# A chunked recurrence and an MLP in one kernel: tables of powers applied by TensorE products for two chunks, and a remainder of x taken by a product with minus one

## The chip, the cores and the metric

The kernel runs on one core of one Trainium2 chip. The time is that of one execution on the device, in microseconds (us); a measured time is the median of several executions. The profile is of one execution, and its span is the time from the first to the last instruction.

## The reference, cut to what matters

```python
# r, k, v: (B=4, H=8, S=768, D=48); w in 0.85..0.95 and u: (8, 48)
for t in range(S):
    cur = einsum('bhd,bhe->bhde', u * kt, vt)
    y[:, :, t] = einsum('bhd,bhde->bhe', rt, state + cur)
    state = w * state + einsum('bhd,bhe->bhde', kt, vt)
x = y as (3072 tokens, 384)
h = x @ w_in                      # 384 x 2048
g = max(h, 0) + alpha * min(h, 0)
out = g @ w_out                   # 2048 x 384
```

## The kernel before

The 768 time steps are cut into C = 6 chunks of L = 128 tokens. A chunk of all four batches is NT = 512 columns. Heads are taken in P = 4 pairs q; the two heads of a pair lie on partitions 0 to 47 and 64 to 111 of a 112-row tile.

**The recurrence.** For a pair (c, q) the tiles `r` and `k0` hold r and k with the feature on the partitions and (batch, token) in the free dimension. VectorE multiplies them by rows of powers of w (the tables `W[q]`). Their products per batch give scores; a mask (`copy_predicated`) and a diagonal term (`base`) make the matrix that is multiplied with `v`. The state `T[q]` (feature by feature, per batch) needs k a second time, with the token on the partitions: the tile `k`, shape [128, 2*B, D]. It is loaded from DRAM (`kk<-vkr`) and multiplied on VectorE by a table of powers by token, `scale_k` at L382: `wtok` for chunk 0, `whalf` for the later chunks, which work in two halves of 64 tokens. `token_table` and `half_table` make these tables by ScalarE copies (L275, L292), TensorE transposes (L279, L296) and one VectorE copy (L282, L299). Chunk 0 is handled by `first_chunk`, where `state` issues the load of k (L447), scales it and makes U (L457). The pairs of chunks 1 to 5 are handled by `prepare` and `burst`; `hasty` marks chunk 1. One burst is one block of TensorE work: the earlier pair's output y through the state (L569) and through the scores (L579), then this pair's products (L543, L550); the rest of y's products (`through_scores(1)`) follow after a small ScalarE read, `seen_y` (L592).

**x as two parts.** The MLP runs on fp32r operands, and each operand is split in a high part and the rest: `xh` and `xl` for x, `wh` and `wl` for the weights, `gh` and `gl` for g. In `burst` the function `splits` does this for y by four quarter blocks of 48 partitions by 256 columns: ScalarE copies a block of PSUM to `xh` (L361) and VectorE subtracts, xl = y - xh (L362). Some rows of x are then moved between partitions by small DMAs (`lower`, L350).

**The MLP.** A step is one chunk with one 128-wide slice i of the hidden layer: 9 products of 128 x 512 into a bank (`m_in`, L628), ScalarE and VectorE work for g, gh and gl (L636, L637, L640, L641), and 9 products into three accumulators (`m_out`, L661). The steps run as chunk 0 with slices 0 to 8, chunk 1 with slices 0 to 8, chunk 0 and then chunk 1 with slices 9 to 15, and then chunks 2 to 5. Each slice of weights comes as one load of 768 KB into `wraw`, which has two buffers, and is unpacked and split by ScalarE (L326, L336) and VectorE (L328, L330, L333, L337); L330 and L333 are the last to read `wraw`, and the load two slices on waits for them.

**The order.** Every piece of work is registered with an engine, an estimated time, what it reads and writes and a rank; `in_order` plays this through as a list schedule and gives one order for all engines. The engines run their queues in that order. SP issues all loads, in order as well. Five PSUM banks are handed out by the schedule, three more are the accumulators; other tiles rotate over a fixed number of buffers (raw 6, v 4, kk 3). Where the schedule leaves TensorE a gap in the start-up, short products on `ident` (`warm`, L721) are put in.

Of the kernel before, what the change touches and what calls it, by code (L numbers as in the profile page):

```python
# [18 lines left out]
L = 128  # L19
# [48 lines left out]
class Plan:  # L68
# [108 lines left out]
def rwkv_prelu_kernel(ctx: ExitStack, tc, rk, vkr, wP, uP, u, wall, alpha, w, r_all, k_all, v_all, oT):  # L177
# [13 lines left out]
    def sb(shape, name, bufs, dt=F32):  # L191
        return plan.buf(lambda: wk.tile(shape, dt, name=name, bufs=bufs), name, bufs)
# [16 lines left out]

    W = [fixed([112, L + 1], f"W{m}") for m in range(P)]  # L210
    w128, unit = fixed([112, P], "w128"), fixed([112, 65], "unit")
    wtok = sb([128, H, D], "rr", 1)

    T = [None] * P

    uw = fixed([112, P, 2], "uw")
    wh, wl = ([fixed([128, 2 * NK, 128], f"{n}{i}", F32R) for i in range(NF)] for n in ("wh", "wl"))
    flag = fixed([1, 1], "flag", I32)

    bank = pb([128, NT], "acc2")  # L220
    plan.banks += [ps.tile([128, NT], F32, name=f"bank{i}") for i in range(5)]

    def psum(group=None, bufs=0):
        return Bank(plan, group, bufs)


    def half(h):
        return slice(HI * (h % 2), HI * (h % 2) + D)
# [40 lines left out]
            out=w128()[:, m:m + 1], in0=t()[:, 128:129], in1=t()[:, 128:129], op=ALU.mult), r=[t], w=[(w128, m)],  # L269
            rank=-31)  # L270

    def token_table():
        rows, pt = sb([112, P, L], "g", 3), psum()
        for m in range(P):
            add("ACT", 0.4, lambda m=m: nc.scalar.activation(  # L275
                rows()[:, m], W[m]()[:, L - 1::-1], AF.Copy, scale=w128()[:, m:m + 1]), r=[W[m], (w128, m)],
                w=[(rows, m)], rank=-30)
        for m in range(P):
            add("PE", 0.15, lambda m=m: nc.tensor.transpose(  # L279
                pt()[:, 128 * m:128 * m + 112], rows()[:, m], ident()[0:112, 0:112]),  # L280
                r=[(rows, m), ident], w=[(pt, m)], rank=-30)
        add("DVE", 0.4, lambda: nc.vector.tensor_copy(  # L282
            wtok().rearrange("p (m g) e -> p m g e", g=2),
            pt()[:, :].rearrange("p (m g e) -> p m g e", m=P, g=2)[:, :, :, 0:D]), r=[pt], w=[wtok], rank=-30)

    def half_table():

# [99 lines left out]

    def first_chunk(q):
        r, k0 = (sb([112, B, L], *(("o", 2) if q == P - 1 else ("raw", 6))) for _ in range(2))
        v, k = sb([128, 2 * B, D], "v", 4), sb([128, 2 * B, D], "kk", 3)  # L390
        n = 2 * B * D
        inputs(0, q, r, k0, v, k, -99 + 0.1 * q)
        first_k.append(k0)
        first_v.append(v)
        if q == P - 1:
            raw_weights(0, -97, [k0])
            raw_weights(1, -95, [v])
        for j, (t, tab) in enumerate(((r, lambda: W[q]()[:, None, 0:L]), (k0, lambda: W[q]()[:, None, L - 1::-1]))):
            add("DVE", 0.72, lambda t=t, tab=tab: nc.vector.tensor_tensor(
                out=t(), in0=t(), in1=tab().broadcast_to([112, B, L]), op=ALU.mult),  # L400
                r=[W[q]], w=[t], rank=10 * q + j - 90)
        cu = sb([128, 2, B], "cu", 2)
        diagonal(q, r, k0, cu, bank, slice(8 * q, 8 * q + 8), (bank, q), 10 * q - 88, -90.2 + q, -51 + q)

        A = [psum() if q % 2 == 0 else pb([128, NT], f"acc{g}") for g in range(2)]

        def scores():
            for b in range(B):
                for g in range(2):
                    nc.tensor.matmul(A[g]()[:, b * L:(b + 1) * L], k0()[half(g), b], r()[half(g), b], start=(b == 0),  # L410
                                     stop=(b == B - 1), skip_group_check=True)

        add("PE", 1.1, scores, r=[r, k0], w=A, rank=10 * q - 90)
        base = [sb([128, B, L], "gl" if q % 2 else "base", 3) for _ in range(2)]
        for g in range(2):
            for b in range(B):
                add("ACT", 0.39, lambda g=g, b=b: nc.scalar.activation(
                    base[g]()[:, b], ident(), AF.Copy, scale=cu()[:, g, b:b + 1]), r=[cu, ident], w=[(base[g], b)],
                    rank=-50.9 + q)
        for g in range(2):  # L420
            add("DVE", 0.75, lambda g=g: nc.vector.copy_predicated(
                base[g](), strict()[:, None, :].broadcast_to([128, B, L]),
                A[g]()[:, :].rearrange("p (b t) -> p b t", b=B)), r=[strict, A[g]], w=[base[g]],
                rank=10 * q - 76 + g)
        y = psum()

        def out():
            for b in range(B):
                for g in range(2):
                    rows, x = (slice(0, HI) if g == 0 else half(g)), g * B + b  # L430
                    nc.tensor.matmul(y()[rows, b * L:(b + 1) * L], v().rearrange("p x e -> p (x e)")[
                        :, x * D:x * D + rows.stop - rows.start], base[g]()[:, b], start=b == 0,
                        stop=b == B - 1, skip_group_check=True)

        add("PE", 1.0, out, r=[v] + base, w=[y], rank=10 * q - 90)
        h, l, kx = x_tiles(0, q)
        if q < P - 1:
            splits(kx, h, l, y, lambda: y()[0:112, :], slice(0, 112), slice(0, NT), [0, 2, 3, 4, 5], 0.6, q - 51.2)
        if q:
            lower(0, q - 1)  # L440
        if q == P - 1:
            for g in range(2):
                splits(kx, h, l, y, lambda g=g: y()[half(g), :], half(g), slice(0, NT), [2 + 2 * g, 3 + 2 * g], 0.6,
                       q - 51.2)

        def state():
            load(k, lambda: nc.sync.dma_start(k().rearrange("p x e -> p (x e)"), vkr[0, q, :, n:2 * n]), 192,  # L447
                 -20 + q, [first_v[P - 1]])
            U = psum()
            add("DVE", 0.56, lambda: scale_k(k, wtok, q), r=[wtok], w=[k], rank=0.5 * q - 1)  # L450

# [12 lines left out]
        return state  # L464
# [20 lines left out]
    def prepare(c, q, at):  # L485
        hasty = c == 1
        r, k0 = (sb([112, B, L], "raw", 6) for _ in range(2))
        v, k = sb([128, 2 * B, D], "v", 4), sb([128, 2 * B, D], "kk", 3)
        n, early = 2 * B * D, at - 7
        inputs(c, q, r, k0, v, k, early)  # L490
        load(k, lambda: nc.sync.dma_start(k().rearrange("p x e -> p (x e)"), vkr[c, q, :, n:2 * n]), 192,
             early + 0.1 * q + 0.2)


        for t, tab in ((r, lambda: W[q]()[:, None, 0:HI]), (k0, lambda: W[q]()[:, None, L - 1:HI - 1:-1])):
# [20 lines left out]
        for g in range(2):  # L516
            for b in range(B):
                add("ACT", 0.32, lambda g=g, b=b: nc.scalar.activation(  # L518
                    base()[:, g, b], ident2(), AF.Copy, scale=cu()[:, g, b:b + 1]), r=[cu, ident2],
                    w=[(base, (g, b))], rank=at - 0.9)  # L520
        add("DVE", 0.56, lambda: scale_k(k, whalf, q), r=[whalf], w=[k], rank=at - 1.6)
        return r, k0, v, k, base

    def burst(i, was, at):
# [222 lines left out]

    for m in range(P):
        table(m)
    states = [first_chunk(q) for q in range(P)]  # L750
    token_table()
    for state in states:
        state()
    half_table()
# [145 lines left out]
```

## Time and profile before

| what | value |
|---|---|
| median of 3 runs | 497.99 us (497.15 to 499.1) |
| profiled execution, its own time | 496.93 us |
| its span | 495.1 us |
| TensorE busy | 474.7 us, 96% of the span |
| VectorE busy | 323.0 us, 65% |
| ScalarE busy | 242.0 us, 49% |
| GpSimd busy | 43.7 us, 9% |
| mean granted TensorE clock | 0.986 |

The shares are means over a start-up in which no MLP product runs yet, a stretch with all weight slices to unpack, and a long rest, so they are to be read by stretch. Product rows are pipelined: a row of 128 x 512 has a duration of some 0.39 us while nine of them take 2.04 us.

### The profile page before, as it was taken

How to read it: one execution, taken by the hardware profiler on the slowest of the kernel's cores; microseconds unless marked ns; L12 is line 12 of the kernel's file. 1: busy time of each engine (PE TensorE's matmuls, PEld its weight loads, DVE VectorE, ACT ScalarE, POOL GpSimd, SP SyncE). 2: the span in 40 equal slices, each digit the busy share in tenths (PEclk: the TensorE clock that was granted, in tenths of full speed). 3: DMA queues.
4: the chain of work that ended last, by engine and by line, in shares of the span. 5: the costliest groups of instructions: out<-in, count | busy, mean ns of one | idle time of the engine just before them, and what ended most of it. 6: DMA issues, size and time to landing. Idle time of an engine off the chain costs nothing.

```text
span 495.1 us, 11103 instructions
## 1 busy us (share of the span) xinstructions
PE 474.7 (96%) x4563; PEld 389.8 (79%) x4563; DVE 323.0 (65%) x550; ACT 242.0 (49%) x565; POOL 43.7 (9%) x49
## 2 busy tenths in 40 slices
PE   8979958999999999999999999999999999999994
PEld 6857747788888888888888888888888888888883
DVE  7889999999976678556648546747535434333331
ACT  3957647666664455525535635535633333423332
POOL 2000100001312111000311110211000000000000
PEclk9889989999999999999999999999999999999998
DMA  7964576475153253313212223212120000100001
GB/s 215 312 212 138 160 225 187 133 216 180 53 157 121 71 177 104 127 63 77 94 36 86 83 69 84 86 36 70 58 60 1 1 1 1 64 0 2 0 1 68
DMA packets 24888, 47.39 MB, mean 96 GB/s; under 512 B 4096, under 2 KB 12416, under 8 KB 24832
## 3 DMA queue, kind: packets, MB, share of 16 engines
q1 hardware_dynamic: 24832, 46.62, 30.6%
q8 instruction: 38, 0.62, 0.6%
q14 instruction: 18, 0.15, 0.1%
HBM read 37.96 MB, written 6.29 MB: 89 GB/s over the span
## 4 chain that ended last, share of the span: by engine, by line
PE 78%; DVE 11%; DMA 5%; ACT 2%; issue 2%; SPq 1%; DVEq 0%; ACTq 0%
PE acc L661 35%; PE bank L628 34%; DMA wraw<-wall 2%; PE bank L569 2%; PE bank L579 2%; DVE wx L333 2%; PE bank L550 2%; PE bank L543 1%; DVE wl L337 1%; DVE g L637 1%; DVE gl L641 1%; DMA v<-vkr 1%; DMA kk<-vkr 1%; DVE wx L330 1%; DVE raw L496 1%
## 5 line engine op out<-in xcount | busy, mean ns | idle before, releaser
L637 DVE SCALAR_TENSOR_TENSOR g<-bank,alph,g 128x512 f32<-128x512 f32 x96 | 71.9, 749 | 107.7 <-ACT g L636 106.2
L636 ACT ACTIVATE g<-bank 128x512 f32<-128x512 f32 x96 | 57.3, 596 | 139.7 <-PE bank L628 139.6
L628 PE MATMUL bank<-xh,wh 128*128 128x512 f32 x288 | 114.6, 398 | 6.0 <-ACT wx L326 5.0
L628 PE MATMUL bank<-xh,wl 128*128 128x512 f32 x288 | 113.2, 393 | 0.1
L628 PE MATMUL bank<-xl,wh 128*128 128x512 f32 x288 | 113.0, 393 | 0.0
L640 ACT ACTIVATE gh<-g 128x512 fp32r<-128x512 f32 x96 | 60.6, 631 | 72.0 <-DVE g L637 71.9
L641 DVE TENSOR_TENSOR gl<-g,gh 128x512 fp32r<-128x512 f32 x96 | 71.5, 745 | 36.8 <-ACT gh L640 36.8
L661 PE MATMUL acc<-gh,wh 128*128 128x512 f32 x288 | 83.5, 397 | 1.0 <-ACT gh L640 1.0
L661 PE MATMUL acc<-gh,wl 128*128 128x512 f32 x288 | 81.7, 391 | 0.0
L661 PE MATMUL acc<-gl,wh 128*128 128x512 f32 x288 | 81.2, 389 | 0.0
L628 PEld LDWEIGHTS bank<-xh,wh 128*128 128x128 f32 x288 | 54.8, 190 | 18.0 <-issue 6.5
L628 PEld LDWEIGHTS bank<-xh,wl 128*128 128x128 f32 x288 | 54.9, 191 | 11.6 <-DVE wl L337 0.6
L628 PEld LDWEIGHTS bank<-xl,wh 128*128 128x128 f32 x288 | 54.7, 190 | 11.6
L661 PEld LDWEIGHTS acc<-gl,wh 128*128 128x128 f32 x288 | 54.1, 188 | 11.4
L661 PEld LDWEIGHTS acc<-gh,wl 128*128 128x128 f32 x288 | 53.9, 188 | 11.5
L661 PEld LDWEIGHTS acc<-gh,wh 128*128 128x128 f32 x288 | 52.6, 188 | 12.5 <-ACT gh L640 1.3
L507 POOL TENSOR_TENSOR rr<-rr,kk 128x384 f32<-128x384 f32 x16 | 20.6, 1290 | 295.4 <-DMA kk<-vkr 217.3
L518 ACT ACTIVATE base<-ident,cu 128x64 f32<-128x64 f32 x160 | 41.5, 337 | 1.4 <-DVE cu L513 1.2
L362 DVE TENSOR_TENSOR xl<-bank,xh 48x256 fp32r<-48x256 f32 (+2 forms) x85 | 37.2, 437 | 2.8 <-ACT xh L361 1.0
L361 ACT ACTIVATE xh<-bank 48x256 fp32r<-48x256 f32 (+2 forms) x85 | 33.2, 391 | 5.9 <-PE bank L579 2.4
L496 DVE TENSOR_TENSOR raw<-raw,W 112x512 f32<-112x512 f32 x40 | 26.2, 680 | 0.3 <-DMA raw<-rk 0.3
L509 POOL TENSOR_TENSOR rr<-rr,utab 128x384 f32<-128x384 f32 x16 | 20.4, 1273 | 1.3
(93 smaller groups left out, 366.9 us busy)
## 6 DMA issues: line engine op xcount, KB each, us to landing
wraw<-wall SPq DMA_DIRECT2D x16, 768.0 KB, 4.7
raw<-rk SPq DMA_DIRECT2D x46, 224.0 KB, 4.2
v<-vkr SPq DMA_DIRECT2D x24, 192.0 KB, 4.4
kk<-vkr SPq DMA_DIRECT2D x24, 192.0 KB, 3.7
rr<-vkr SPq DMA_DIRECT2D x16, 192.0 KB, 2.5
oT<-o SPq DMA_DIRECT2D x12, 256.0 KB, 2.1
oT<-g SPq DMA_DIRECT2D x6, 256.0 KB, 2.6
xh<-xh SPq DMA_DIRECT2D x36, 32.0 KB, 2.3
```

The source lines that it names most:

```text
L361: add("ACT", us, lambda: nc.scalar.activation(to(h), view(), AF.Copy), r=[src], w=refs(h), rank=rank)
L362: add("DVE", us + 0.1, lambda: nc.vector.tensor_tensor(out=to(l), in0=view(), in1=to(h), op=ALU.subtract), r=[src] + refs(h), w=refs(l), r ...
L496: add("DVE", 0.72, lambda t=t, tab=tab: nc.vector.tensor_tensor(out=t().rearrange("p b (j t) -> p (b j) t", j=2), in0=t().rearrange("p b ( ...
L507: add("POOL", 1.2, lambda: nc.gpsimd.tensor_tensor(out=rt(), in0=rt(), in1=k(), op=ALU.mult), r=[k] + ([wh[12]] if c == 2 else []), w=[rt] ...
L509: add("POOL", 1.2, lambda: nc.gpsimd.tensor_tensor(out=rt().rearrange("p (g b) e -> p g b e", g=2), in0=rt().rearrange("p (g b) e -> p g b ...
L518: add("ACT", 0.32, lambda g=g, b=b: nc.scalar.activation(base()[:, g, b], ident2(), AF.Copy, scale=cu()[:, g, b:b + 1]), r=[cu, ident2], w ...
L628: nc.tensor.matmul(hp()[:, :], a[i]()[:, k], x[c]()[:, k], start=(k == 0 and j == 0), stop=(k == NK - 1 and j == 2))
L636: add("ACT", 0.6, lambda: nc.scalar.activation(g(), hp()[:, :], AF.Copy), r=[hp], w=[g], rank=n - 100)
L637: add("DVE", 0.75, lambda: nc.vector.scalar_tensor_tensor(out=g(), in0=hp()[:, :], scalar=alph()[:, i:i + 1], in1=g(), op0=ALU.mult, op1=A ...
L640: add("ACT", 0.64, lambda: nc.scalar.activation(gh(), g(), AF.Copy), r=[g], w=[gh], rank=n - 100)
L641: add("DVE", 0.73, lambda: nc.vector.tensor_tensor(out=gl(), in0=g(), in1=gh(), op=ALU.subtract), r=[g, gh], w=[gl], rank=n - 99)
L661: nc.tensor.matmul(banks[k](), a[i]()[:, NK + k], x(), start=(begin and j == 0), stop=(end and j == 2))
```

## The change

For chunks 0 and 1 the tile `k` is no longer loaded and scaled. Eight diagonal matrices `turn[n][m]` of 112 x 112 are made by GpSimd from the identity (n = 0 with w to the 128th, n = 1 with w to the 64th). In `by_tokens` four TensorE products with `k0` as the stationary and a `turn` as the moving operand give the scaled k by tokens in a PSUM bank, and ScalarE copies 384 of its columns to `k`. `token_table` and its tile `wtok` are gone; `half_table` stays for chunks 2 to 5.

For the pairs of chunk 1 (`c0 > 1` is false) the rest of x is no longer VectorE's: ScalarE copies the four blocks to `xh`, four TensorE products with a matrix of minus ones on the diagonal subtract them in the PSUM bank itself (`less`), and ScalarE copies the four blocks again, to `xl`.

The tile `kk` has 4 buffers, not 3, and the constructor is given dynamic_dma_scratch_size=4096.

```diff
-    wtok = sb([128, H, D], "rr", 1)
+    minus = fixed([128, HI], "minus")
+    turn = [fixed([112, P, 112], f"turn{n}") for n in range(2)]
...
-    def token_table():
...
+    def turns():
         for m in range(P):
+            for n in range(2):
+                def diag(m=m, n=n):
+                    nc.gpsimd.tensor_scalar(turn[n]()[:, m], ident()[0:112, 0:112],
+                                            w128()[:, m:m + 1] if n == 0 else W[m]()[:, L:L + 1], None, op0=ALU.mult)
+
+                add("POOL", 0.35, diag, r=[ident, (w128, m) if n == 0 else W[m]], w=[(turn[n], m)],
+                    rank=10 * m - 60 + 45 * n)
+        add("ACT", 0.2, lambda: nc.scalar.activation(minus(), ident2(), AF.Copy, scale=-1.0), r=[ident2], w=[minus],
+            rank=-9)
+
+    def by_tokens(q, n, k0, k, rank, copy_rank):
+        pt = psum()
+
+        def products():
+            for b in range(B):
+                nc.tensor.matmul(pt()[:, b * L:b * L + 112], k0()[:, b], turn[n]()[:, q], start=(b == 0),
+                                 stop=(b == B - 1), skip_group_check=True)
+
+        add("PE", 0.8, products, r=[k0, (turn[n], q)], w=[pt], rank=rank)
+        add("ACT", 0.5, lambda: nc.scalar.activation(
+            k().rearrange("p (g b) e -> p g b e", g=2),
+            pt()[:, :].rearrange("p (b g e) -> p b g e", b=B, g=2)[:, :, :, 0:D], AF.Copy), r=[pt], w=[k],
+            rank=copy_rank)
... first_chunk
+        by_tokens(q, 0, k0, k, 10 * q - 85, -50.5 + q)
... state
-            load(k, lambda: nc.sync.dma_start(k().rearrange("p x e -> p (x e)"), vkr[0, q, :, n:2 * n]), 192,
-                 -20 + q, [first_v[P - 1]])
-            add("DVE", 0.56, lambda: scale_k(k, wtok, q), r=[wtok], w=[k], rank=0.5 * q - 1)
... prepare
-        load(k, lambda: nc.sync.dma_start(k().rearrange("p x e -> p (x e)"), vkr[c, q, :, n:2 * n]), 192,
-             early + 0.1 * q + 0.2)
+        if not hasty:
+            load(k, ...)                       # as before
...
+        if hasty:
+            by_tokens(q, 1, k0, k, at - 3, at - 1.6)
+        else:
+            add("DVE", 0.56, lambda: scale_k(k, whalf, q), r=[whalf], w=[k], rank=at - 1.6)
... burst
-                    splits(...)                # for every chunk
+            if c0 > 1:                         # splits as before
+            else:
+                def copy(t, rank):
+                    for g, o, n0 in places:
+                        add("ACT", 0.38, lambda g=g, o=o, n0=n0: nc.scalar.activation(
+                            to(t, g, n0), y[g]()[half(o), 0:2 * L], AF.Copy), r=[y[g]],
+                            w=[(t, (kx, 2 + 2 * g + (o != g)))], rank=rank)
+
+                def less():
+                    for g, o, n0 in places:
+                        nc.tensor.matmul(y[g]()[half(o), 0:2 * L], minus()[half(g), 0:D], to(h, g, n0).bitcast(F32),
+                                         start=False, stop=True, skip_group_check=True)
+
+                copy(h, at - 0.3)
+                add("PE", 0.5, less, r=[minus] + [...], w=y, rank=at - 100)
+                copy(l, at - 0.29)
```

## Rows read from the trace of the kernel before

**Rows 1.** Busy time of each engine by stretch, a stretch far behind the start.
```profile
200.00:300.00 100.00, 100.00 (x1153) 82.80 (x1152) 62.56 (x112) 47.81 (x119) 13.51 (x10) 1.00 0.26 80
```

**Rows 2.** The same view, 31 to 86 us: PE, PEld, DVE, ACT, POOL, PEclk, DMA, GB/s.
```profile
31.00:34.40 3.40, 0.66 (x17) 0.60 (x17) 3.04 (x5) 0.61 (x2) 0.00 (x0) 0.95 0.95 304
34.40:37.10 2.70, 2.70 (x7) 2.12 (x8) 1.89 (x3) 1.56 (x3) 0.00 (x0) 0.50 0.93 286
37.10:44.70 7.60, 6.70 (x92) 5.23 (x90) 6.99 (x13) 5.97 (x15) 0.00 (x0) 0.98 0.42 140
44.70:63.30 18.60, 17.76 (x333) 14.17 (x333) 18.48 (x30) 11.86 (x33) 2.27 (x2) 1.00 0.50 143
63.30:68.40 5.10, 0.10 (x2) 0.06 (x1) 5.07 (x10) 3.40 (x7) 0.00 (x0) 0.98 0.74 238
68.40:71.50 3.10, 3.10 (x8) 2.42 (x9) 3.01 (x8) 0.00 (x0) 0.00 (x0) 0.50 0.96 288
84.00:86.10 2.10, 0.81 (x41) 0.51 (x31) 2.07 (x3) 1.61 (x5) 0.00 (x0) 1.00 0.71 178
```

**Rows 3.** The view of waits for TensorE, 28 to 145 us: total, times, longest.
```profile
PE bank L628 <- ACT wx L326: 5.0, 1, 5.0
PE bank L579 <- ACT seen_y L592: 0.8, 2, 0.6
```

**Rows 4.** The view of waits for SP's queue, first 100 us.
```profile
SPq L308 <- DVE wx L333: 35.8, 8, 9.4
```

**Rows 5.** Groups of VectorE instructions by line and shape, 23 to 63.3 us.
```profile
L382 DVE TENSOR_TENSOR kk<-kk,rr 128x384 f32<-128x384 f32 x4 | 2.2, 552 | 0.0
L362 DVE TENSOR_TENSOR xl<-bank,xh 48x256 fp32r<-48x256 f32 x4 | 1.7, 422 | 0.1
L382 DVE TENSOR_TENSOR kk<-kk,whalf 128x384 f32<-128x384 f32 x3 | 1.6, 550 | 0.0
...
L282 DVE COPY rr<-bank 128x384 f32<-128x384 f32 x1 | 0.5, 543 | 0.0
```

**Rows 6.** The same view, 63.3 to 100.9 us.
```profile
L362 DVE TENSOR_TENSOR xl<-bank,xh 48x256 fp32r<-48x256 f32 x12 | 5.1, 422 | 0.3
```

**Rows 7.** DMA in the start-up: busy time by stretch, 10 to 20 us.
```profile
10.00:20.00 10.00, 10.00 (x112) 8.98 (x110) 8.56 (x22) 8.76 (x29) 0.00 (x0) 0.83 1.05 319
```

**Rows 8.** The timeline, loads as SP issues them: start, duration.
```profile
13.96 3.54 SPq L447 DMA_DIRECT2D kk<-vkr  x3
...
28.38 0.73 SPq L350 DMA_DIRECT2D xh<-xh  x1
```

**Rows 9.** The timeline, VectorE and GpSimd at 56 to 61 us.
```profile
56.20 0.55 DVE L328 TENSOR_SCALAR wx<-wx 128x768 uint32<-128x768 uint32 x1
...
58.79 1.07 POOL L507 TENSOR_TENSOR rr<-rr,kk 128x384 f32<-128x384 f32 x1 [54.99 <-DMA kk<-vkr]
...
58.91 1.36 DVE L328 TENSOR_SCALAR wx<-wx 128x768 uint32<-128x768 uint32 x1
```

**Rows 10.** The timeline, the instructions nearest to the new ones.
```profile
1.13 0.29 POOL L243 TENSOR_SCALAR_AFFINE_SELECT ident<-g 128x128 f32<-128x128 f32 x1
...
11.17 1.16 PE L410 MATMUL acc<-raw 48*128 48x128 f32 x16
...
21.18 0.58 PE L279 MATMUL bank<-ident,g 112*128 112x112 f32 x4
...
50.60 0.66 PE L569 MATMUL bank<-raw,T 48*48 48x64 f32 x32
```

**Rows 11.** Groups of ScalarE instructions by line and shape, 9 to 100.9 us.
```profile
L326 ACT ACTIVATE wx<-wraw 128x768 f32<-128x768 f32 x11 | 9.9, 900 | 5.3 <-DMA wraw<-wall 5.1
...
L361 ACT ACTIVATE xh<-bank 48x256 fp32r<-48x256 f32 x16 | 6.1, 378 | 1.7 <-PE bank L579 1.4
...
L361 ACT ACTIVATE xh<-bank 112x512 fp32r<-112x512 f32 x3 | 1.8, 587 | 1.2 <-PE bank L431 1.2
...
L275 ACT ACTIVATE g<-W,w 112x128 f32<-112x128 f32 x4 | 1.3, 387 | 0.0
```

More of the change, by code (lines that the diff above doesn't have):

```diff
@@ L270, in table @@
             rank=-31)
-    def token_table():
-        rows, pt = sb([112, P, L], "g", 3), psum()
+    def turns():
         for m in range(P):
[L275 to L284, printed above, removed]
+            for n in range(2):
[15 more added lines that the diff above has]
+            k().rearrange("p (g b) e -> p g b e", g=2),
+            pt()[:, :].rearrange("p (b g e) -> p g b e", b=B, g=2)[:, :, :, 0:D], AF.Copy), r=[pt], w=[k],
+            rank=copy_rank)
     def half_table():
@@ L389, in first_chunk @@
         r, k0 = (sb([112, B, L], *(("o", 2) if q == P - 1 else ("raw", 6))) for _ in range(2))
-        v, k = sb([128, 2 * B, D], "v", 4), sb([128, 2 * B, D], "kk", 3)
-        n = 2 * B * D
+        v, k = sb([128, 2 * B, D], "v", 4), sb([128, 2 * B, D], "kk", 4)
         inputs(0, q, r, k0, v, k, -99 + 0.1 * q)
@@ L487, in prepare @@
         r, k0 = (sb([112, B, L], "raw", 6) for _ in range(2))
-        v, k = sb([128, 2 * B, D], "v", 4), sb([128, 2 * B, D], "kk", 3)
+        v, k = sb([128, 2 * B, D], "v", 4), sb([128, 2 * B, D], "kk", 4)
         n, early = 2 * B * D, at - 7
         inputs(c, q, r, k0, v, k, early)
-        load(k, lambda: nc.sync.dma_start(k().rearrange("p x e -> p (x e)"), vkr[c, q, :, n:2 * n]), 192,
-             early + 0.1 * q + 0.2)
+        if not hasty:
+            load(k, lambda: nc.sync.dma_start(k().rearrange("p x e -> p (x e)"), vkr[c, q, :, n:2 * n]), 192,
+                 early + 0.1 * q + 0.2)
         for t, tab in ((r, lambda: W[q]()[:, None, 0:HI]), (k0, lambda: W[q]()[:, None, L - 1:HI - 1:-1])):
@@ L520, in prepare @@
                     w=[(base, (g, b))], rank=at - 0.9)
-        add("DVE", 0.56, lambda: scale_k(k, whalf, q), r=[whalf], w=[k], rank=at - 1.6)
+        if hasty:
+            by_tokens(q, 1, k0, k, at - 3, at - 1.6)
+        else:
+            add("DVE", 0.56, lambda: scale_k(k, whalf, q), r=[whalf], w=[k], rank=at - 1.6)
         return r, k0, v, k, base
@@ L611, in burst, with to @@
             h, l, kx = x_tiles(c0, q0)
-            for g in (1, 0):
-                for o in (g, 1 - g):
-                    n0 = 0 if o == g else 2 * L
+            places = [(g, o, 0 if o == g else 2 * L) for g in (1, 0) for o in (g, 1 - g)]
+            if c0 > 1:
+                for g, o, n0 in places:
                     splits(kx, h, l, y[g], lambda g=g, o=o: y[g]()[half(o), 0:2 * L], half(g),
                            slice(n0, n0 + 2 * L), [2 + 2 * g + (o != g)], 0.38, at - 0.3)
+            else:
+                def to(t, g, n0):
+                    return t()[half(g), n0:n0 + 2 * L] if kx is None else t()[half(g), kx, n0:n0 + 2 * L]
+                def copy(t, rank):
[4 more added lines that the diff above has]
+                def less():
+                    for g, o, n0 in places:
+                        nc.tensor.matmul(y[g]()[half(o), 0:2 * L], minus()[half(g), 0:D], to(h, g, n0).bitcast(F32),
+                                         start=False, stop=True, skip_group_check=True)
+                copy(h, at - 0.3)
+                add("PE", 0.5, less, r=[minus] + [(h, (kx, 2 + 2 * g + (o != g))) for g, o, _ in places], w=y,
+                    rank=at - 100)
+                copy(l, at - 0.29)
             if q0:
@@ L749, in rwkv_prelu_kernel @@
         table(m)
+    turns()
     states = [first_chunk(q) for q in range(P)]
-    token_table()
     for state in states:
@@ L891 @@
     }
-    nc = bacc.Bacc("TRN2", target_bir_lowering=False, num_devices=1)
+    nc = bacc.Bacc("TRN2", target_bir_lowering=False, num_devices=1, dynamic_dma_scratch_size=4096)
     args = [nc.dram_tensor(n, a.shape, mybir.dt.from_np(a.dtype), kind="ExternalInput").ap() for n, a in arrays.items()]
```

## The prediction

> **What bounds the kernel now.** I read the table of busy time by stretch first, because a mean of 96% for TensorE hides where the other 4% is. Far behind the start TensorE is busy in all of 100 us [rows 1]; nothing that another engine gains there shortens the run, and the change touches nothing there. What can be won lies before. I cut the stretch from 31 to 86 us at TensorE's gaps [rows 2]. TensorE stands idle for 3.40 - 0.66 = 2.74 us up to 34.4, for 0.90 up to 44.7, 0.84 up to 63.3, 5.00 up to 68.4 and 1.29 around 85. After the first and the fourth gap the granted clock reads 0.50, the lower of the two levels (1.2 for 2.4 GHz), for 2.7 and 3.1 us; half of these, 1.35 and 1.55, are lost too. All together that is 10.77 + 2.90 = 13.67 us. After gaps of about 1.3 us or less the rows show 1.00 or nearly so.
>
> Next I asked what these gaps wait for. The longest is put down to ScalarE's unpacking of a weight slice [rows 3], but in the same rows VectorE is busy for 5.07 of the 5.10 us, and for 18.48 of the 18.60 before: unpacking is late because VectorE is late. The view of SP's waits says how it feeds back: the weight load waits up to 9.4 us for VectorE's L333, the last reader of the buffer [rows 4]. So in this stretch VectorE sets the pace, and TensorE has room only in its gaps. The first gap is another kind: VectorE has pauses there (0.36, 0.81 and 0.61 us idle in the first three rows), and the DMA share is 0.95 [rows 2].
>
> **The change, part by part.**
>
> *VectorE, before 63.3 us.* Removed are the four multiplications by wtok, three of the four by whalf, the copy that makes wtok, and four subtractions [rows 5]: 2.2 + 1.6 + 0.5 + 1.7 = 6.0 us. VectorE's instructions start slightly before the end of the one ahead, so I take off 0.6. Its own 1.8 us of pauses up to 44.7 swallow that much, since there it waits for data and not for itself. 6.0 - 0.6 - 1.8 = 3.6 us arrive at the long gap, which shrinks from 5.0 to 1.4. A gap so short is not followed by the lower clock in these rows, so 1.55 us go as well. Gain 5.15; bounds 0 (another cause holds the same gap) and 6.55.
>
> *DMA at the start.* Three loads of 192 KB for chunk 0 are issued from 13.96 us [rows 8], in a stretch where DMA is saturated at 319 GB/s [rows 7]: 3 x 0.197 MB / 319 GB/s = 1.85 us. The small DMAs that complete x, issued behind them up to 28.38 us and later [rows 8], end the first gap. I count 1.85 of 2.74 us as won, and half of the 1.35 us of low clock: 2.5. Bounds 0 and 4.09. The fourth load, and the four of chunk 1, free SP and DMA later; I give them nothing of their own.
>
> *VectorE, after 63.3 us.* Twelve subtractions, 5.1 us [rows 6], and one multiplication go. The gaps of 0.90, 0.84 and 1.29 us sum to 3.03; I count half, 1.5, bounds 0 and 3.03.
>
> *TensorE, products for k.* Four products of 112 x 128 with 112 columns are like the four transposes of L279, 0.58 us with the last one's tail [rows 10]. At 0.55 the four sets of chunk 1 cost 2.2 us, on TensorE's own path. At the lower clock they would cost twice that, so the bounds are 1.9 and 4.4. Those of chunk 0 fall in the start-up where short filler products run now; they cost nothing as long as there is filler, and 2.2 us without it.
>
> *TensorE, products with minus one.* Four products of 48 x 48 with 256 columns per pair. No row shows them. L569 runs 32 products of 48 x 48 with 64 columns in 0.66 us [rows 10], where neighbours use different quarters of the array: half as many columns, 0.33 us. If none overlaps, L410 gives the other end: 16 products of 128 columns, two row halves in turn, in 1.16 us, so 0.145 us for 128 columns alone and 1.16 for four times 256. The four new products lie in four different quarters, so they are nearer to L569; I take 0.45, four times 0.45 = 1.8 (bounds 1.3 and 4.6).
>
> *The new wait.* These products stand in TensorE's queue and wait for four ScalarE copies of 0.378 us [rows 11], and all MLP products behind wait with them. The order puts other products in between. The nearest wait is TensorE's for the small ScalarE read, 0.8 us in two times among four bursts of chunk 1 [rows 3], 0.2 a burst: 0.8 for four. Bounds 0 and 4 x 1.5 = 6.0 us, all four copies waited out each time.
>
> *ScalarE.* Sixteen copies to xl are 16 x 0.378 = 6.0 us more, but ScalarE is busy for only 11.86 of 18.60 us before the long gap [rows 2]. They take the place of VectorE's late subtractions, so the banks of y are not held longer. The copies of 384 columns lie between 0.378 (256) and 0.587 (512), about 0.48; in chunk 0 four make 1.9 us against 1.5 for the four that leave with the table [rows 11]. ScalarE is busy for 8.76 of 10 us there [rows 7], so I count 0.5 us of delay for these (bounds 0 and 1.9).
>
> *GpSimd.* Eight `turn` tiles at about 0.29 us (an instruction over 128 x 128 [rows 10]) are 2.3 us of work on an idle engine. I cost them at nothing: they run before k is needed, and k of chunk 0 only feeds the state. What speaks against that: beside GpSimd's work at 58.8 us VectorE's L328 took 1.36 us, not 0.55 [rows 9], 0.8 more. The Trainium skill, "GPSIMD Engine Reference", section "Key points", has the rule: GpSimd shares its SBUF interfaces with VectorE and collides with instructions that have two SBUF inputs or use both ports; the trace agrees with the 1.36 us. By that rule `turns` would slow VectorE's first multiplications, which have two SBUF inputs.
>
> *Sum.* Gains 5.15 + 2.5 + 1.5 = 9.15; costs 2.2 + 1.8 + 0.8 + 0.5 = 5.3; net 3.85, rounded to 3.9 us. The profiled execution took 496.93 us (its span 495.1 and 1.83 around it), which becomes 493.0. The median of the runs is 1.06 us above it, so the forecast against the median is 497.99 - 3.9 = 494.1 us. The larger buffer count of `kk` costs nothing in time, and for the smaller DMA scratch no row shows a use.
>
> **The rivals.**
>
> *The gap stays, with another cause.* When VectorE comes earlier, the weight slices wait for their loads instead: DMA is at 0.74 and 0.96 in and after the long gap [rows 2]. For it: three waits of ScalarE for `wraw` already sum to 5.1 us [rows 11]. Against it: SP's load is itself waiting for VectorE. If about 3.9 us less are recovered, gains just pay the new products: 498 us.
>
> *TensorE waits for ScalarE (slower).* The order was made with estimates. If a weight copy of 0.9 us [rows 11] and the four copies stand in front of each set of products with minus one, each waits 0.9 + 1.5 = 2.4 us: 9.6 instead of 0.8, 8.8 more than my sum, so 4.9 us slower: 502.9. It turns the sign from a wait of 0.2 + 3.9 / 4 = 1.2 us a pair on, and the result is over 0.5% slower from 1.8 us on. For it: TensorE's queue is in order, and both copies of a pair now go through ScalarE. Against it: ScalarE is idle for a third of the time.
>
> *GpSimd holds VectorE in the start-up.* 1.07 us of GpSimd work cost 0.8 us, so 2.3 us cost 1.7; if all lands on the path to the first MLP product, the gain is 3.9 - 1.7 = 2.2: 495.8. The skill's rule above is this mechanism. Against it: only some of the tiles meet such instructions, and VectorE's lead is not always on the path.
>
> *Everything comes back.* All 13.67 us less the costs of 5.3 make 8.4: 489.6. For it: VectorE is the one cause behind most gaps. Against it: the first gap is DMA's.
>
> **How the numbers follow.** My forecast has 0.48 (its own range 491.5 to 496.0, from the bounds of the wait and the recovered part of the long gap), the unchanged gap 0.22, the wait for ScalarE 0.15, GpSimd 0.05, everything back 0.10. Runs of before spread by 0.4%, so about 0.5% (2.5 us) can be told from no change. Faster than 495.5: 0.40 of my 0.48, 0.10, and 0.05 of the others, 0.55. Slower than 500.5: 0.14 of the ScalarE wait and 0.03 of the unchanged gap with dearer products, 0.17. The rest, 0.28, is the same. A range of 489.5 to 499.5 holds the forecast, everything back, GpSimd and nearly all of the unchanged gap, 0.82.
>
> **What the profile after would show.** The gap at 63 us shrunk to about 1.4 us, with no 0.50 clock behind it, and SP's longest wait for L333 under 6 us: VectorE was the cause. If the gap is as long and VectorE has pauses in it, a load was. L628 of the first slices starting earlier than now: DMA at the start. TensorE's waits for L361 or the new copies: under 0.5 us a pair by my sum, over 1.2 by the slower rival. Sets of four products for k over 0.6 us, or of minus one over 0.5, mean mis-sized terms. I am wrong in kind if the stretch after 101 us changes in length, since nothing there is touched.

## The result

The median of 15 runs is 493.94 us (488.17 to 496.57); before, in 15 runs, 497.89 us (495.23 to 500.39). The ratio is 0.9899, with a 95% interval from 0.9868 to 0.993: 3.5 to 6.6 us less. Medians are of all runs; the ratios leave out those more than 1.5% above their kernel's fastest (three of the 15 here, one in e3 and four in e11), which count as slow. The profiled execution took 494.9 us, its span is 493.2 us, 1.9 us shorter than that of before. So the two executions with a trace show half of what the medians show; that of before lies 0.96 us under its median and that of after 0.96 us above.

Most of that other half is the clock of the start-up. Two stretches, before and then after (columns as in [rows 2], the clock third from the end):

```profile
0.00:25.00 25.00, 23.19 (x214) 19.63 (x215) 20.20 (x45) 15.94 (x49) 2.71 (x17) 0.93 0.88 262
20.00:144.00 124.00, 112.17 (x1238) 90.35 (x1236) 117.69 (x188) 80.78 (x189) 10.49 (x8) 0.97 0.55 168
```

```profile
0.00:25.00 25.00, 22.86 (x190) 19.81 (x191) 18.96 (x42) 14.24 (x45) 9.21 (x25) 0.86 0.78 239
20.00:144.00 124.00, 119.76 (x1324) 95.25 (x1321) 111.96 (x172) 92.33 (x219) 13.55 (x10) 1.00 0.50 159
```

In its first 25 us the traced execution of after loses 1.7 us more to the lower clock than that of before; e9 below shows that one and the same start-up can run with more or less of it. Without these 1.7 us the spans differ by 3.6, near the medians. Between 20 and 144 us the lower clock takes 3.5 us before and nothing after.

The runs without a trace say the same. Each has its span and its mean granted clock on record, and span times (1 - clock) is an estimate, somewhat high, of what the lower clock took. Its mean is 9.4 us in 82 runs of before and 4.6 in the 12 runs of after that are in the ratio; what is left of the span is 486.9 and 486.6 us. So by this estimate nearly the whole gain is time at the lower clock. The idle time that the change fills is paid back by its products.

After, busy time by stretch at the places of [rows 2], and two stretches further on (total, then PE, PEld, DVE, ACT, POOL, PEclk, DMA, GB/s):

```profile
31.50:34.40 2.90, 2.90 (x33) 2.33 (x30) 2.59 (x5) 2.41 (x5) 0.00 (x0) 1.00 0.99 326
...
44.70:63.30 18.60, 17.86 (x332) 14.18 (x330) 18.42 (x30) 15.17 (x37) 2.75 (x2) 1.00 0.47 147
63.30:68.40 5.10, 5.10 (x30) 3.58 (x31) 5.07 (x10) 4.92 (x18) 0.00 (x0) 1.00 0.92 282
68.40:71.50 3.10, 3.10 (x118) 2.46 (x116) 2.09 (x4) 3.06 (x8) 0.00 (x0) 1.00 0.45 112
...
80.00:84.00 4.00, 3.04 (x18) 1.67 (x17) 4.00 (x6) 2.06 (x7) 0.00 (x0) 1.00 1.03 339
84.00:89.40 5.40, 4.28 (x19) 3.20 (x19) 3.46 (x6) 3.87 (x7) 0.00 (x0) 1.00 0.70 229
```

The 5 us gap of TensorE between 63.3 and 68.4 is gone, the first gap too, and the clock stays at 1.00 behind both. Two gaps of about 1 us are new at 81 and 89 us. The waits say the same; after, for TensorE, 20 to 150 us (total, times, longest):

```profile
PE bank L661 <- DVE wl L350: 2.1, 2, 1.1
PE bank L483 <- DVE g L478: 1.3, 3, 0.7
PE acc L694 <- ACT cu L487: 0.5, 2, 0.3
PE bank L444 <- ACT kk L294: 0.3, 1, 0.3
```

(L661 was L628 and L350 was L337.) No wait for L637, the copies around the product with minus one, is among them. After, SP's longest wait for the last read of the raw weights is 6.2 us, not 9.4 [rows 4], and VectorE's longest waits are for a load, which it did not wait for between 20 and 100 us before. Two of them stand in its queue in front of the last step of a weight slice (L350), for which TensorE waits in the two new gaps:

```profile
SPq L321 <- DVE wx L346: 31.7, 7, 6.2
```

```profile
DVE raw L507 <- DMA raw<-rk: 4.6, 3, 2.4
```

```profile
79.94 0.69 DVE L507 TENSOR_TENSOR raw<-raw,W 112x512 f32<-112x512 f32 x1 [2.37 <-DMA raw<-rk]
80.55 0.95 DVE L350 TENSOR_TENSOR wl<-wx,wh 128x768 fp32r<-128x768 f32 x1
...
86.95 0.69 DVE L507 TENSOR_TENSOR raw<-raw,W 112x512 f32<-112x512 f32 x1 [1.91 <-DMA raw<-rk]
...
88.22 0.95 DVE L350 TENSOR_TENSOR wl<-wx,wh 128x768 fp32r<-128x768 f32 x1
```

What the gain was paid with stands in the timeline of after (start, duration). Eight rows are one set of four products:

```profile
17.43 2.05 PE L290 MATMUL bank<-turn,raw 112*128 112x112 f32 x8
...
31.55 0.50 PE L661 MATMUL bank<-xh,wh 128*128 128x512 f32 x1
...
48.84 1.15 PE L290 MATMUL bank<-turn,raw 112*128 112x112 f32 x8
...
49.91 0.65 PE L643 MATMUL bank<-xh,minus 48*48 48x256 f32 x8
...
65.61 1.07 PE L643 MATMUL bank<-xh,minus 48*48 48x256 f32 x8
```

The first MLP product starts at 31.55 us; before it was at 29.43:

```profile
29.43 0.50 PE L628 MATMUL bank<-xh,wh 128*128 128x512 f32 x1
```

Far behind the start nothing changes in length: the 181st of the 864 products into the accumulators (L661, then L694) starts at 151.8 us before and at 149.8 after, and 343.3 and 343.4 us follow to the end of the span.

### The profile page after: what moved, and what is told of

It reads as the page before. It is cut to its first block, busy times and chain, and to the rows that moved or that the text cites. A ratio compares the mean times of both kernels' runs of the same rounds, so it can differ in the third digit from the quotient of the medians.

```text
span 493.2 us, 11205 instructions
## 1 busy us (share of the span) xinstructions
PE 479.9 (97%) x4617; PEld 393.1 (80%) x4617; DVE 310.8 (63%) x525; ACT 249.8 (51%) x586; POOL 53.3 (11%) x57
## 4 chain that ended last, share of the span: by engine, by line
PE 86%; DVE 6%; ACT 3%; DMA 3%; issue 1%; SPq 0%; DVEq 0%; ACTq 0%
PE acc L694 38%; PE bank L661 37%; DMA raw<-rk 3%; PE bank L583 2%; PE bank L593 2%; PE bank L564 2%; PE bank L557 1%; DVE wx L346 1%; PE bank L444 1%; DVE wl L350 1%; DVE g L670 1%; PE acc L483 1%; PE bank L422 1%; PE bank L290 1%; DVE g L478 1%
## 5 line engine op out<-in xcount | busy, mean ns | idle before, releaser
L661 PE MATMUL bank<-xh,wl 128*128 128x512 f32 x288 | 112.3, 390 | 2.1 <-DVE wl L350 2.1
L661 PE MATMUL bank<-xh,wh 128*128 128x512 f32 x288 | 113.2, 393 | 0.0
L661 PE MATMUL bank<-xl,wh 128*128 128x512 f32 x288 | 112.1, 389 | 0.0
L674 DVE TENSOR_TENSOR gl<-g,gh 128x512 fp32r<-128x512 f32 x96 | 69.8, 727 | 37.9 <-ACT gh L673 37.2
L694 PE MATMUL acc<-gh,wh 128*128 128x512 f32 x288 | 83.4, 397 | 0.5 <-ACT cu L487 0.5
L694 PE MATMUL acc<-gh,wl 128*128 128x512 f32 x288 | 81.9, 391 | 0.0
L694 PE MATMUL acc<-gl,wh 128*128 128x512 f32 x288 | 81.6, 390 | 0.0
L661 PEld LDWEIGHTS bank<-xh,wl 128*128 128x128 f32 x288 | 54.1, 188 | 13.8 <-DVE wl L350 2.9
L661 PEld LDWEIGHTS bank<-xh,wh 128*128 128x128 f32 x288 | 54.1, 188 | 12.8 <-issue 1.0
L661 PEld LDWEIGHTS bank<-xl,wh 128*128 128x128 f32 x288 | 54.1, 188 | 11.3
L694 PEld LDWEIGHTS acc<-gh,wl 128*128 128x128 f32 x288 | 53.8, 188 | 11.5
L694 PEld LDWEIGHTS acc<-gl,wh 128*128 128x128 f32 x288 | 53.8, 188 | 11.3
L694 PEld LDWEIGHTS acc<-gh,wh 128*128 128x128 f32 x288 | 52.7, 188 | 11.9 <-ACT gh L673 0.7
L518 POOL TENSOR_TENSOR rr<-rr,kk 128x384 f32<-128x384 f32 x16 | 23.4, 1460 | 260.6 <-DMA kk<-vkr 182.2
L375 DVE TENSOR_TENSOR xl<-bank,xh 48x256 fp32r<-48x256 f32 (+2 forms) x69 | 30.4, 441 | 3.3 <-ACT xh L374 2.0
L374 ACT ACTIVATE xh<-bank 48x256 fp32r<-48x256 f32 (+2 forms) x69 | 27.2, 394 | 4.5 <-PE bank L444 2.4
```

Of the source, the lines that this page charges most:

```text
L374: add("ACT", us, lambda: nc.scalar.activation(to(h), view(), AF.Copy), r=[src], w=refs(h), rank=rank)
L375: add("DVE", us + 0.1, lambda: nc.vector.tensor_tensor(out=to(l), in0=view(), in1=to(h), op=ALU.subtract), r=[src] + refs(h), w=refs(l), r ...
L518: add("POOL", 1.2, lambda: nc.gpsimd.tensor_tensor(out=rt(), in0=rt(), in1=k(), op=ALU.mult), r=[k] + ([wh[12]] if c == 2 else []), w=[rt] ...
L661: nc.tensor.matmul(hp()[:, :], a[i]()[:, k], x[c]()[:, k], start=(k == 0 and j == 0), stop=(k == NK - 1 and j == 2))
L674: add("DVE", 0.73, lambda: nc.vector.tensor_tensor(out=gl(), in0=g(), in1=gh(), op=ALU.subtract), r=[g, gh], w=[gl], rank=n - 99)
L694: nc.tensor.matmul(banks[k](), a[i]()[:, NK + k], x(), start=(begin and j == 0), stop=(end and j == 2))
```

## The experiments

Ratios are those of a kernel's runs to the runs of the kernel before, with the 95% interval. The "gaps" are those of TensorE over 0.3 us between 20 and 144 us, added up from the one profiled execution; "low clock" is the estimate from above, span times (1 - clock), as a mean of the runs in the ratio; the last column is when the seventh load of raw weights is issued. Code in the cuts is shortened.

| kernel | median us | ratio | gaps us (longest) | low clock us | seventh load us |
|---|---|---|---|---|---|
| before | 497.8 to 498.4 | 1 | 11.4 (5.0) | 9.4 | 62.6 |
| the change | 493.94 | 0.9899 [0.9868, 0.993] | 3.5 (1.1) | 4.6 | 53.1 |
| e1, less only | 492.51 | 0.9878 [0.9837, 0.9919] | 5.1 (1.4) | 5.4 | 58.0 |
| e2, tokens only | 494.74 | 0.9914 [0.9882, 0.9945] | 5.5 (1.4) | 5.9 | 57.3 |
| e3, chunk 1 only | 492.40 | 0.9874 [0.9824, 0.9924] | 1.0 (1.0) | 4.8 | 53.2 |
| e5, VectorE's work back | 495.06 | 0.9949 [0.9917, 0.998] | 2.9 (0.7) | 6.0 | 54.9 |
| e8, buffers only | 497.23 | 0.9971 [0.9936, 1.0007] | 8.0 (3.4) | 8.5 | 62.2 |
| e9, cut in place | 496.45 | 0.9973 [0.9939, 1.0007] | 10.9 (4.5) | 8.5 | 60.8 |
| e10, before, other order | 502.38 | 1.0088 [1.0055, 1.0121] | 11.8 (3.2) | 11.3 | 61.6 |
| e11, changed, other order | 495.32 | 0.9915 [0.9874, 0.9955] | 4.2 (2.0) | 6.3 | 50.8 |
| e12, before, three raw | 497.92 | 1.0006 [0.998, 1.0031] | 9.5 (2.8) | 9.4 | 53.1 |
| e13, before, unpack earlier | 497.18 | 0.9988 [0.9956, 1.0019] | 9.8 (2.9) | 8.8 | 55.7 |
| e14, changed, three raw | 492.80 | 0.9893 [0.9849, 0.9936] | 2.3 (1.2) | 5.6 | 51.1 |
| e15, chunk 1, three raw | 498.13 | 1.0000 [0.9965, 1.0034] | 4.2 (1.7) | 6.8 | 45.9 |

### The parts one at a time

e1 keeps only the product with minus one (and the side edits of e8):

```diff
-        by_tokens(q, 0, k0, k, 10 * q - 85, -50.5 + q)
+        load(k, ...); scale_k(k, wtok, q)       # chunk 0, with token_table, as before
-        if hasty: by_tokens(q, 1, k0, k, at - 3, at - 1.6)
+        load(k, ...); scale_k(k, whalf, q)      # chunk 1 as before
```

> The whole change moved the ratio to 0.990 and the profiled span by 1.9 us. This run keeps only the product with minus one (chunk 0 and 1 load and scale k as before; no diagonal tables). My theory (VectorE's backlog makes the long gap) says: 6.8 of the 11.7 us that leave VectorE leave here, the price on TensorE is about 3 us (32 rows, 0.6 to 1.0 us a pair), so the gap at 63 us shrinks to 2 us or less and the time is 494 to 497, half of the gain or less. Rival (the loads are what counts): the gap stays over 4 us and the time is that of before or up to 3 us worse.

Measured 0.9878: all of the gain, more than I expected, with no gap over 1.41 us from 20 us on. The first gap is still there, in two parts (1.41 us at 31 and 1.23 at 33), and the lower clock behind it.

e2 is the other half; the subtractions stay with VectorE for every pair of `burst`:

```diff
-            if c0 > 1:
+            if c0 > 0:
```

> Only k by tokens for both chunks; the rest of x of chunk 1 stays VectorE's. Theory: 4.9 us leave VectorE and 1.6 MB leave DMA, eight sets at 1.1 us come to TensorE, four of them on its path (4.4 us); the gap at 63 us is halved, the time is 495 to 498. Rival (the loads are what counts): as fast as the whole change, 493 to 495.

Measured 0.9914, again nearly all of it, in the range of the rival and faster than my theory. The two halves do not add up: each alone takes the long gap away, and with it most of the low clock (5.4 and 5.9 us, 4.6 with both). That the second half's own products eat what it could still win is my reading, not shown apart. So neither "only the loads count" nor "the gap shrinks in proportion" holds.

e3 has both for chunk 1 and leaves chunk 0 as it was:

```diff
-        by_tokens(q, 0, k0, k, 10 * q - 85, -50.5 + q)
+        load(k, ...); scale_k(k, wtok, q)       # with token_table, without turn[0]
```

> The whole change for chunk 1, chunk 0 as before (k loaded, token table made by ScalarE, TensorE and VectorE). In the changed kernel the first MLP product starts at 31.6 us, 2.1 later than before, with four sets of products for k of chunk 0 in front of it, 2.05 us each at the lower clock. If these are the cause, the first MLP product starts at about 29.5 us again and the time is 491 to 493, faster than the whole change. Rival: the loads of chunk 0 delay the small DMAs of x as in the kernel before, the gap at 31 us comes back with the lower clock (4.1 us lost), and the time is 495 to 497.

The time is as I expected, 0.9874, but not for the reason that I gave: the first MLP product starts at 31.72 us without chunk 0's products in front of it (one set of chunk 1's is there, 1.1 us). It starts at 33.48 in e8 and 32.77 in e10 too, which have none at all. What the start goes with is the granted clock of the first 25 us: 1.00 in e9 and e11 (28.15 and 28.50 us), 0.93 in the kernel before (29.43), 0.86 in the change and in e3, and 0.80 in e8 and e10. The others lie within 1.3 us of this row, and only e15 is far off (0.93, and 33.20 us). Neither the order nor the products for k are needed to explain it. And the first gap came back only in part with chunk 0's loads: 0.95 us at 33 us, and no lower clock. So these loads alone do not make it.

### The amount of VectorE's work, or its order

e5 puts sixteen VectorE instructions, that nothing waits for, where the subtractions were:

```diff
                 copy(h, at - 0.3)
+                for g, o, n0 in places:
+                    add("DVE", 0.48, lambda: nc.vector.tensor_tensor(
+                        out=junk(), in0=alike()[0:48, 0:288], in1=alike()[0:48, 0:288], op=ALU.subtract),
+                        r=[(h, (kx, 2 + 2 * g + (o != g))), alike], w=[junk], rank=at - 0.3)
```

> The whole change, and sixteen VectorE instructions of 48 x 288 elements that no other work waits for, at the place and rank of the removed subtractions; they compute nothing that is used. Theory (VectorE sets the pace): the gap of TensorE around 63 to 68 us or another of 3 us or more is back with VectorE busy all through it, and the time rises by 3 to 6 us, to 496 to 500. Rival (DMA or ScalarE sets the pace after the change): no more than 1 us, 493 to 495.

0.9949 lies between: by the ratios half of the gain is lost, by the medians a quarter (1.1 us above the changed kernel), with intervals that overlap. But no gap of 3 us came back, and the gaps sum to 2.9 us. VectorE's time alone does not make the long gap.

e8 has the side edits alone:

```diff
-sb([128, 2 * B, D], "kk", 3)
+sb([128, 2 * B, D], "kk", 4)
-bacc.Bacc("TRN2", ..., num_devices=1)
+bacc.Bacc("TRN2", ..., num_devices=1, dynamic_dma_scratch_size=4096)
```

> The kernel before with only the fourth buffer of kk and the smaller DMA scratch; no operation is added or removed, but the list schedule gives another order. My theory (work taken from VectorE is the gain) says 496 to 499, no difference from before. Rival (the fourth buffer, or the new order that comes with it, is the gain): 492 to 495.

No difference (0.9971, an interval that holds 1), and a gap of 3.36 us. The side edits are not the gain.

e9 is the sharpest. It is the kernel before with the same sequence on every engine's queue; sixteen VectorE instructions only have a quarter of their columns:

```diff
-    nc.vector.tensor_tensor(out=k4, in0=k4, ...)                      # scale_k, 0.55 us
+    nc.vector.tensor_tensor(out=k4[:, :, 0:1], in0=k4[:, :, 0:1], ...) # 0.25 us, chunks 0 and 1
-    in1=tab().broadcast_to([112, 2 * B, HI])                           # r and k0, 0.68 us
+    in1=tab().broadcast_to([112, 2, HI])                               # 0.28 us, chunk 1
```

> The kernel before with the same order of all instructions on all engines, but sixteen VectorE multiplications cut to a quarter of their columns: the eight that scale k and the eight of r and k0 of chunk 1 (three quarters of these rows stay unscaled, so the output is not the reference's). About 8 us of VectorE's work go, no other engine gets any and no load changes. Theory (VectorE's backlog makes the long gap): the gap of 5.0 us shrinks below 1.5 us and the time falls by 4 to 8 us, to 490 to 494. Rival (the order, not the amount of VectorE's work, makes the gap): the gap stays above 3 us and the time within 2 us of before, 496 to 498.

The gap stayed at 4.5 us and the time at 0.9973:

```profile
PE bank L634 <- DVE T L611: 4.5, 1, 4.5
```

By the rows, 8 x 0.30 + 8 x 0.40 = 5.6 us left VectorE, all but 0.3 of it before the gap ends. That is less than the 8 that I announced, but the long gap should still have shrunk by more than half. The trace of e9 shows why it didn't. ScalarE, then VectorE, from 53 us on:

```profile
54.77 0.91 ACT L326 ACTIVATE wx<-wraw 128x768 f32<-128x768 f32 x1 [1.90 <-DMA wraw<-wall]
55.70 0.60 ACT L642 ACTIVATE g<-bank 128x512 f32<-128x512 f32 x1
```

```profile
56.34 0.75 DVE L643 SCALAR_TENSOR_TENSOR g<-bank,alph,g 128x512 f32<-128x512 f32 x1 [0.75 <-ACT g L642]
57.00 0.95 DVE L330 SCALAR_TENSOR_TENSOR wx<-wraw,wx 128x768 uint32<-128x768 uint32 x1
57.87 0.56 DVE L328 TENSOR_SCALAR wx<-wx 128x768 uint32<-128x768 uint32 x1
58.34 0.69 DVE L647 TENSOR_TENSOR gl<-g,gh 128x512 fp32r<-128x512 f32 x1
58.94 1.76 DVE L333 SCALAR_TENSOR_TENSOR wx<-wraw,wx 128x768 uint32<-128x768 uint32 x1
60.63 1.77 DVE L330 SCALAR_TENSOR_TENSOR wx<-wraw,wx 128x768 uint32<-128x768 uint32 x1
...
65.38 0.96 DVE L337 TENSOR_TENSOR wl<-wx,wh 128x768 fp32r<-128x768 f32 x1 [0.17 <-ACT wh L336]
```

ScalarE's queue holds the unpacking of the sixth slice in front of g. It waits 1.90 us for that slice's load; g waits behind it, VectorE waits 0.75 us for g, and only then comes the unpacking of the fifth and the sixth slice, with two instructions stretched from 0.95 to 1.76 us where GpSimd works. What VectorE had gained it spent waiting: from 20 us to the end of the gap it idles for 2.0 us in the kernel before, and for 6.4 us over the same instructions in e9. The load of the sixth slice is issued 2.1 us earlier than before (47.53 and 49.63 us), but ScalarE gets it only 0.8 us earlier (54.77 and 55.55). By this trace, with the queues in that order, the load and g set the time of the gap.

e9 shows one thing more. Up to 22 us its engines run the same instructions as in the kernel before; yet the clock reads 1.00 from 10 to 20 us, where [rows 7] has 0.83, and the first MLP product starts 1.28 us earlier. The lower clock of the start-up differs between executions of the same instructions.

### Other orders, other buffers

e10 and e11 change one number: chunk 1's bursts are due earlier, in the kernel before and in the changed one.

```diff
-        at = {1: 0.5 + 1.5 * q, 2: 17.0 + 3.2 * q}.get(...)
+        at = {1: 0.2 + 1.5 * q, 2: 17.0 + 3.2 * q}.get(...)
```

> The kernel before, with the due time of chunk 1's four bursts set 0.3 steps earlier (0.2 instead of 0.5): the same operations in another order. Theory: the gap moves but its cause stays, 496 to 500. Rival (the order of before is an unlucky one, and any other is better): 492 to 495 with no gap over 2 us.

> The changed kernel with the same earlier due time (0.2 instead of 0.5). Theory: within 2 us of the changed kernel, 492 to 496, and below the kernel before with that due time by 3 us or more. Rival (the order decides): the two kernels with that due time lie within 1.5 us of each other, or the changed one is above.

An order alone is worth 0.9%: 502.38 us in e10, with another long gap, 3.2 us at 93 us. But in that order too the change wins, and more: 495.32 us, 7.1 us less. The gain is not the luck of one order.

From e9 I formed a second theory: a loop through the two buffers of raw weights sets the pace, and the change only loosens it. In the table the long gap goes with a late seventh load. e12 gives `wraw` three buffers (and takes the smaller DMA scratch); e13 gives VectorE's unpacking a lower rank. Neither takes any work from VectorE.

```diff
-sb([128, 2 * DM, 2], "wraw", 2, U32)                # e12
+sb([128, 2 * DM, 2], "wraw", 3, U32)
-rank=need - 2 - 60 * (i == 0)                       # e13, L328, L330, L333, L337
+rank=need - 3 - 60 * (i == 0)
```

> The kernel before with three buffers for the raw weights in place of two (and the smaller DMA scratch, which makes room). Second theory, from the cut in place: the pace of the stage is a loop, in which the load of slice i+2 waits for VectorE's last read of slice i, that read stands in an order behind other work, and the load takes 5 to 7 us. In all kernels with a gap at 63 us the seventh load is issued at 61 to 63 us, in the faster ones at 51 to 58. With a third buffer that load no longer waits for the fifth slice: issued before 56 us, the gap below 2 us, the time 492 to 495, with all of VectorE's work left in place. First theory (the amount of VectorE's work): 496 to 499.

> The kernel before with one number changed: VectorE's unpacking of the weight slices has a rank lower by one (need - 3 in place of need - 2), so that the order puts it in front of some of the work on x and on the states of chunk 1. Not one instruction is added or removed. Second theory (the place of the fifth slice's last read in VectorE's order): the seventh load is issued 4 us earlier or more, the gap at 63 us is below 2 us, the time 492 to 496. First theory (the amount): 496 to 500.

The second theory fell. The seventh load did come earlier, at 53.1 and 55.7 us, and the gaps are still 9.5 and 9.8 us in sum: the longest are 2.8 us at 68 and 2.9 at 32, and others of 1.2 to 1.8 us. Both times are those of before. TensorE's idle time moves, but in the kernels that keep all of VectorE's work its sum stays between 8 and 12 us.

e14 and e15 are the changed kernel and e3 with that third buffer.

> The changed kernel with three buffers for the raw weights. If the loop through the weight loads still sets part of the time after the change (two waits for the unpacked weights, 2.1 us in all, and VectorE's waits for loads, 4.6 us, stand in its profile), 490 to 493. If what is left is the products' own time and the start-up, 493 to 495.

> The change for chunk 1 alone (chunk 0 loads and scales k as before) with three buffers for the raw weights: the version that the runs so far point to. It was 492.4 with two buffers, with only 2 us of gaps left in its profile; with the third 490 to 492.5 if the load loop still counts, 492 to 494 if not.

e14 is no faster than the change (0.9893 beside 0.9899). e15 missed by far: 498.13 us, though two buffers gave 492.4. There the slower rival of my prediction happened, once. e15, busy time by stretch around 86 us, and the wait that belongs to it:

```profile
80.00:85.80 5.80, 5.80 (x87) 3.70 (x87) 4.86 (x9) 2.85 (x9) 0.00 (x0) 1.00 0.89 272
85.80:87.60 1.80, 0.11 (x3) 0.08 (x4) 0.89 (x2) 1.74 (x4) 0.00 (x0) 1.00 0.97 353
87.60:94.00 6.40, 6.24 (x19) 4.03 (x20) 4.79 (x7) 4.84 (x10) 0.00 (x0) 0.56 0.96 295
```

```profile
PE bank L661 <- ACT xh L655: 1.9, 2, 1.7
```

(L661 here is the product with minus one.) TensorE waits 1.7 us for ScalarE's copies, and behind that the clock reads 0.56 over 6.4 us, which costs another 6.4 x 0.44 = 2.8 us. The span of this execution is 7.0 us longer than e3's (495.8 and 488.8); these 4.5 us are most of that, and the first MLP product starts 1.5 us later. Why it does is open.

## Why the prediction was right, point by point

The forecast of 494.1 us met the median of 493.94. Its terms did less well. Against the two traces:

- **Long gap, 5.15 us: right, a little small.** 5.00 shrank to 0.73 us (62.4 to 63.1), and the 1.55 us of low clock went: 5.8. But the way that I gave, 6.0 us taken from VectorE and 3.6 arriving at the gap, is not how it works. e9 takes 5.6 us in the same order, and the gap loses 0.5. In all runs that lost the long gap the work had gone and the queues had been put in order again without it.
- **First gap, 2.5 us: the reason failed.** The gap of 2.74 us shrank to 0.30, with no low clock behind, 3.8 us. In e3, with the three loads that I blamed, it is down to 0.95 too. In e13, whose first product starts at 30.4 us, it is 2.9 us. What makes it is open.
- **Small gaps, 1.5 us: next to nothing.** From 37 us on, the gaps over 0.3 us other than the long one sum to 0.90 + 0.45 + 0.39 + 0.64 + 0.65 = 3.0 before and 0.33 + 0.31 + 0.96 + 1.12 = 2.7 after, two of them new, behind weights that come late.
- **The start, 2.1 us later: not foreseen.** 1.7 of these are the lower clock of this execution's start-up, 0.4 are left for the change.
- **Products for k, 2.2 us: mis-sized by two.** A set takes about 1.1 us, not 0.55. I read the four rows of L279 as four products, which they are, but transposes; an ordinary f32 product stands in the trace as two rows. L410 shows it: eight products in the code, 16 rows [rows 10]. One of the four sets lies before the first MLP product, so 3 x 1.1 = 3.3 us are on the path. Of chunk 0's four sets only the one at 17.43 us ran at the lower clock, not each as I wrote for e3; at an equal clock they moved the start by 0.4 us at most.
- **Products with minus one, 1.8 us: too small for the same reason.** 0.65, 1.07, 0.65 and 0.65 us, 3.0 together; in the second, the weight loads waited 0.37 and 0.27 us for ScalarE's copies. The quarters do overlap: eight rows of 256 columns took 0.65 us, and the 32 rows of 64 columns of L569, as many columns in all, took 0.66 [rows 10]. I had counted four rows.
- **The new wait, 0.8 us: none in TensorE's own waits.** What there is lies in the 1.07 us just named. It is real in e15, at 1.9 us and its low clock.
- **ScalarE in the start-up, 0.5 us: not seen as such.** Of the later start at most the 0.4 us that the clock leaves can be its.
- **GpSimd at nothing: right.** The four tiles of chunk 1 took 4.32 us together, the others 2.18, much longer than my 0.29 each, but in time.

Sum on the traces: 5.8 + 3.8 + 0.3 - 2.1 - 3.3 - 3.0 = 1.5 us, beside 1.9 in the spans; without the 1.7 us of the start-up's clock 3.2, beside 3.6. My gains were about as large as these, my costs too small. Of the 3.6 us the low clock between 20 and 144 us is 3.5, for which I had counted 2.2; idle time won and products added nearly cancel, and I had a net gain of 1.7 us there. The number was met partly by luck, by errors that cancel.

The rival that the gap stays for another cause was wrong for the long gap but right in kind for what is left: both new gaps wait for unpacked weights, which are late because VectorE had stood 2.37 and 1.91 us waiting for a load in front of them. The rival with GpSimd failed in its direction. Beside the first four tiles VectorE's first multiplications took no longer than before (0.69 us at the median), while GpSimd's instructions took 1.09 us. The other four took 0.56 beside VectorE's work on PSUM banks (`copy_predicated`) and short instructions; VectorE was about as busy there. After, groups of GpSimd, first 20 us:

```profile
L277 POOL TENSOR_SCALAR turn<-ident,W 112x112 f32<-112x112 f32 x4 | 4.3, 1094 | 0.1
L277 POOL TENSOR_SCALAR turn<-ident,w 112x112 f32<-112x112 f32 x4 | 2.2, 559 | 5.3 <-DVE w L269 5.3
```

The rule of the Trainium skill that I weighed ("GPSIMD Engine Reference", "Key points") fits the trace in that the two engines got in each other's way; no run has these tiles alone, so the cause of the 1.09 us is argued. Here it was GpSimd that paid, 1.09 us for 0.56; in e9's rows at 59 and 61 us it was VectorE, 1.76 for 0.95, in instructions with two SBUF inputs. (L328 of [rows 9] has one, so that row alone doesn't show which part of the rule applies.)

What is shown: the gain is not in the side edits (e8), not in one lucky order (e10, e11), not in the raw buffers (e12), and either half of the change gives it (e1, e2). Kernels with all of VectorE's work have 8 to 12 us of gaps in five orders (before, e8, e10, e12, e13), lose 8.5 to 11.3 us to the low clock and take 497.2 to 502.4 us. Kernels with work moved or taken from VectorE, and an order made for that, have 1 to 6 us of gaps, lose 4.6 to 6.8 and take 492.4 to 495.3 us but for e15. What stays open is how much of it is VectorE's time and how much the order that a shorter list gives: e5 says that a quarter to a half can be lost by time put back (in an order made for it), e9 that time alone gives at most 0.6%, and both intervals are wide. Open is also whether e1 or e3 is faster than the whole change; their intervals overlap with its own.

## What to carry to other kernels

A gap of one engine behind a busy engine is not yet that engine's fault: take the work out with every queue left in its order, and see whether the gap shrinks. When a schedule makes the order, a change of work is always a change of order too, and orders alone moved this kernel by 0.9%, so a change is tested in two orders. Before two traces are compared term by term, compare the granted clock of a stretch that the change does not touch, and of all runs on record. Count the price of a product by rows per product of the same kind, and a wait of TensorE with the low clock behind it, which can cost more than the wait.

## What the runs showed of the hardware that was not expected

An f32 product that is no transpose (and not fp32r, as the MLP's are) stands as two matmul rows: four products of 112 x 128 by 112 columns as eight rows, 1.15 us at full clock and 2.05 us where the clock reads 0.50. In the start-up of the changed kernel the clock reads 0.50 with TensorE busy throughout:

```profile
14.50:17.50 3.00, 3.00 (x29) 2.44 (x25) 1.79 (x5) 1.14 (x4) 1.19 (x3) 0.50 1.01 346
17.50:19.40 1.90, 1.90 (x8) 1.71 (x8) 1.22 (x3) 0.89 (x2) 0.00 (x0) 0.50 0.93 250
```

e8, without any of the new products, reads 0.50 from 12 to 20 us as well, so it is not the new products that bring it; and e9 and the kernel before, with the same instructions up to 22 us, read 1.00 and 0.83 from 10 to 20. GpSimd's multiplication of a 112 x 112 tile by a column took 0.56 us, twice an `affine_select` of 128 x 128 (0.29), and 1.09 us beside VectorE's multiplications and reciprocals.
